# Three edits of the written order in an attention-and-MoE kernel: a first expert's last products ahead of the next one's transposes, a third expert's last weight loads behind its row transposes, and the last expert's row list held back longer in the plan

## The chip, the cores and the metric

The kernel runs on one core of a Trainium2 chip. The metric is the device time of one execution in microseconds (us); lower is better. The profiled execution has its own time, and a span from the first to the last recorded instruction inside it. Engines: PE is the matrix engine (PEld its weight loads), DVE, ACT and POOL are the vector, scalar and GpSimd engines, SP issues most DMAs.

## The reference

First attention over 8 batches of 8 heads, 576 positions, head size 64, with a causal mask in blocks of 64; then a mixture of experts over the 4608 rows of 512 that come out of it. Cut to what matters:

```python
scores = np.where(block_i >= block_j, scale * q @ k.T, -1e9)
x = softmax(scores) @ v                 # to rows: N=4608, D=512
logits = x @ w_gate                     # 8 experts
order = argsort(-logits.flatten())      # greedy, best pair first
# each row goes to one expert, each expert takes at most N // 8 = 576 rows
for e in range(8):
    h = np.maximum(x[rows_of_e] @ w1[e], 0.0)     # 512 -> 1024
    out[rows_of_e] = h @ w2[e]                    # 1024 -> 512
```

## The kernel before

The program is straight-line code whose order is written by a planner of its own, the class `Sched`. The parts of the work are Python generators that yield (engine, modelled duration, events waited for); the planner starts at each step the task that its model lets start first, by priority, and each start emits the instructions there and then. Engine letters are D, A, T, G, S for DVE, ACT, PE, POOL, SP. So a modelled time (`sc.soft`, `sc.dma`, `sc.ev`) changes no instruction, only the order in which each engine's queue holds them. On the chip every engine runs its queue in that order, and waits on real semaphores.

The first 370 us are attention, which ends with rows of x (an fp16 high part and an fp16 low part, 1024 numbers a row) in DRAM. Then eight experts follow, k = 0 to 7 in the order in which their capacity is filled. For each:

- `route(k)` searches the two bounds of the expert's logits in 14 steps: step t counts on DVE (`jk`, L776 and L777) and ACT (`ja`, L750), sums over the partitions on PE (`tot{k}_{t}`, L791), and goes on in DVE. It ends in masks MM, then `po{k}` on PE (L852 to L859), a row's place in the expert, and `invert`, which turns places into a list of rows: DVE makes h (L870), L (L872), OH (L893), OL (L897), RH (L899, L900), PE makes `pe{k}` (36 products, L908) and `ps{k}` (L915), DVE the index list `ix{k}`. `hold(k)` sets a modelled time before which the planner puts neither po nor pe into PE's order.
- `gather(k)` fetches the 576 rows by five indirect DMAs on POOL (`xg{k}_{m}`, L980; the fifth has 64 rows), and `flip` turns each into X{k}: for k < 2 eight PE transposes into a PSUM tile `xt{k}_{m}` (L990) and two copies (L994, L995), for k > 1 a transposing DMA on SP (L1005).
- `weights(k)` loads eight pieces of 512 KB per expert on SP (`raw{k}_1024_0` to `_3` of w1, `raw{k}_512_0`, `_2`, `_4`, `_6` of w2; L966; six buffers). A piece is scaled on ACT (L945), cut to its fp16 high part on ACT (L949), and the low part `W[:,1]` is made on POOL (L951).
- `ffn(k)` computes h on PE (L1030) as 8 column groups f for rows 0 to 255 and then for the others (`h{k}_{f}_{half}`), each of 12 products: d = 0 to 3, and for each d high by high, high by low rows, low weights by high rows. ACT and DVE cut h into HH and HL (L1016, L1018). Then `y{k}_{m}` (L1055; L1059 for the 64 rows of m = 4), in eight groups of three products of 512 columns (four of six for m = 4), ACT scales it (`yo`, L1038), and POOL scatters it to `out` (L1046). Two scatters write the same DRAM tensor, so that each waits for the landing of the one before.

Instructions of different experts interleave in each queue: the search of expert k+1 or k+2 runs beside the products of k, and the gathers, weight pieces and scatters of neighbouring experts share POOL's and SP's queues.

The lines that a reader needs beside the functions printed below are these of the planner:

```python
def soft(s, t, ev=None, lat=1100):
    s.q = max(s.q, s.now + lat) + t
    if ev:
        s.ev[ev] = s.q + 950
```

Of the kernel before, what the change touches and what calls it, by code (L numbers as in the profile page):

```python
# [16 lines left out]
D, A, T, G, S = "DATGS"  # L17
# [597 lines left out]
class Moe:  # L615
# [269 lines left out]
        yield from s.invert(k,L16,h2)  # L885
    def hold(s,k):

        s.sc.ev['hold',k]=s.sc.now+(8000 if k==s.E-1 else 0)
    def invert(s,k,L16,h2):
        nc=s.nc; rp=s.rp; C=s.C; V=nc.vector; sc=s.sc  # L890
        yield D,440
# [35 lines left out]
    def weights(s,k,eidx):  # L927

        nc=s.nc; wp=s.wp; sc=s.sc
        e=nc.sync.value_load(eidx[0:1,0:1],min_val=0,max_val=s.E-1)  # L930
        yield S,1000,('ffn',k-2)
        W=wp.tile([P,2,4,1024],F16,tag="W1",name=f"W1_{k}"); Y=wp.tile([P,2,8,512],F16,tag="W2",name=f"W2_{k}")
        s.W[k]=(W,Y)
        n=0; t0=sc.now
        def conv(n,raw,hi,lw,ev):
            if k<2 and n<4:
                yield A,947,('wl',k,n)
                nc.scalar.activation(hi,raw,AF.Copy,scale=s.WS)
                yield D,1135,('ix',k),('xm',0,0) if k==0 and n in s.XC else None
                nc.vector.scalar_tensor_tensor(lw,raw,s.WS,hi,op0=OP.mult,op1=OP.subtract)  # L940
            else:
                for h in range(2):
                    x=slice(512*h,512*h+512)
                    yield A,520,('wl',k,n)
                    nc.scalar.activation(raw[:,x],raw[:,x],AF.Copy,scale=s.WS)  # L945
                for h in range(2):
                    x=slice(512*h,512*h+512)
                    yield A,520
                    nc.scalar.activation(hi[:,x],raw[:,x],AF.Copy)  # L949
                yield G,2079  # L950
                nc.gpsimd.tensor_tensor(lw,raw,hi,op=OP.subtract)  # L951
            sc.set(ev)
        for dst,src,nd,wd in ((W,s.w1,4,1024),(Y,s.w2,8,512)):
            g=1024//wd
            for d in range(0,nd,g):
                if n>=6: yield S,25,'hw',('wc',k,n-6)
                elif k>0: yield S,25,'hw',('wc',k-1,n+2),('fl',1) if k==1 and n>=4 else None
                elif n==4:

                    yield G,60,('gi',0)  # L960
                    raw=wp.tile([P,1024],F32,tag="raw",name=f"raw{k}_{wd}_{d}",bufs=6)
                    nc.gpsimd.memset(raw[:,0:1],0.0)
                    yield S,25,'hw'
                else: yield S,25,'hw'
                if k or n!=4: raw=wp.tile([P,1024],F32,tag="raw",name=f"raw{k}_{wd}_{d}",bufs=6)
                nc.sync.dma_start(out=raw.rearrange("p (g f) -> p g f",g=g),in_=src[bass.ds(e,1),d*P:(d+g)*P,:].rearrange("o (g p) f -> p (o g) f",p=P))  # L966
                hi=dst[:,0,d:d+g].rearrange("p g f -> p (g f)"); lw=dst[:,1,d:d+g].rearrange("p g f -> p (g f)")
                sc.dma(1456,('wl',k,n))
                sc.add(conv(n,raw,hi,lw,('wc',k,n)),2,sc.now)
                n+=1  # L970
    WS=32.0; XS=64.0; NWU=8; NWM=0; GW=1; GS=2; XC=()
    def gather(s,k,ix):
        nc=s.nc; fp=s.fp; sc=s.sc
        tl=[]
        for m in range(5):
            n=P if m<4 else 64
            yield G,1038,('ffn',k-2),('xm',k-1,m)
            if m==0: X=s.X[k]=fp.tile([P,8,576],F16,tag="X",name=f"X{k}")
            xg=fp.tile([P,1024],F16,tag="xg",name=f"xg{k}_{m}",bufs=5)
            nc.gpsimd.indirect_dma_start(out=xg[:n],out_offset=None,in_=s.xd,in_offset=bass.IndirectOffsetOnAxis(ap=ix[:n,m:m+1],axis=0))  # L980
            sc.soft(728,('xg',k,m))
            sc.nolat()
            if m==4: sc.set(('gi',k))
            sc.add(s.flip(k,m,n,xg,X),1,sc.now)
# [138 lines left out]
```

## Time and profile before

| what | us |
|---|---|
| three timed executions, median (lowest to highest) | 804.21 (802.95 to 807.38) |
| the profiled execution | 801.86 |
| its span | 800.1 |
| PE busy in it | 717.8 (90%), 6539 products |
| DVE, ACT, POOL busy | 585.0, 545.1, 467.0 |
| DMA | 121.51 MB |

All rows are from the profiled execution, and their starts count from the start of its span. Matrix products are pipelined: a row's duration covers filling and draining, so that successive rows overlap, and the distance of the starts is what a product costs. The granted clock (PEclk) is a share of full speed: 1.00 is 2.4 GHz and 0.50 is 1.2 GHz.

### The profile page before, as it was taken

The page shows a single profiled execution, that of the slowest core. Times are in us where ns is not written, and L with a number is a line of the kernel's source. Part 1 is how long each engine was busy: PE and PEld are TensorE (multiplying, and loading weights), DVE is VectorE, ACT ScalarE, POOL GpSimd, SP SyncE. Part 2 cuts the span into 40 slices and gives each one's busy share as a digit, 9 for nine tenths or more (in the row PEclk, how much of TensorE's full clock was granted, in tenths as well). Part 3 has the DMA queues.
Part 4 walks back from the last instruction along what each step waited for, and adds up shares of the span by engine and source line. Part 5 has one row for each costly group of instructions (what it writes and reads, how often), then busy time and mean ns, then how long its engine had stood idle before and what let it go on. Part 6 is the DMA issues. An engine that isn't in the chain of part 4 may idle for free.

```text
span 800.1 us, 19136 instructions
## 1 busy us (share of the span) xinstructions
PE 717.8 (90%) x6539; PEld 479.6 (60%) x6539; DVE 585.0 (73%) x2395; ACT 545.1 (68%) x1476; POOL 467.0 (58%) x509
## 2 busy tenths in 40 slices
PE   5889998899999999913898999999999999999995
PEld 3666676677767767601644755747557475574752
DVE  6899798988889799488787977969777683730210
ACT  5789888888988888533745859496775947392210
POOL 5788888897889876212324337475471926873001
PEclk9899999999999999955899999999999999999998
DMA  9879999999999991324408049291845819861001
GB/s 203 157 145 179 213 203 209 164 176 204 230 164 222 188 198 35 99 80 133 138 14 294 25 139 231 74 295 42 254 129 184 179 49 273 270 162 40 20 15 45
DMA packets 244305, 121.51 MB, mean 152 GB/s; under 512 B 200816, under 2 KB 227312, under 8 KB 244208
## 3 DMA queue, kind: packets, MB, share of 16 engines
q1 hardware_dynamic: 238320, 101.42, 56.1%
q0 software_dynamic: 5888, 18.88, 7.4%
q8 instruction: 51, 0.84, 0.4%
q14 instruction: 46, 0.38, 0.2%
HBM read 71.32 MB, written 18.87 MB: 113 GB/s over the span
## 4 chain that ended last, share of the span: by engine, by line
PE 58%; DVE 19%; DMA 8%; ACT 8%; issue 3%; POOL 3%; SPq 1%; POOLq 0%; DVEq 0%; ACTq 0%
PE h L1030 23%; PE y L1055 16%; PE psb L463 5%; DVE m L405 5%; PE psb L380 4%; DMA kT<-k 4%; PE psb L498 4%; ACT P L416 4%; DVE kS L350 2%; POOL P L438 2%; PE y L1059 2%; DMA xg<-x,ix 2%; ACT PT L444 2%; DVE jk L776 1%; DMA raw<-in_moe_w_dram 1%
## 5 line engine op out<-in xcount | busy, mean ns | idle before, releaser
L438 POOL TENSOR_TENSOR P<-P,m 128x320 f32<-128x320 f32 (+8 forms) x285 | 209.3, 769 | 48.2 <-DVE m L430 28.4
L1030 PE MATMUL h<-X,W 128*128 128x320 f16 (+3 forms) x1536 | 195.1, 287 | 0.0
L1030 PEld LDWEIGHTS <-W 128*128 128x128 f16 x1536 | 142.2, 98 | 42.7 <-issue 3.1
L416 ACT ACTIVATE P<-psb,m 128x576 f32<-128x576 f32 (+8 forms) x288 | 149.2, 542 | 25.8 <-DVE m L409 19.7
L1055 PE MATMUL y<-W,HH 128*128 128x512 f16 x512 | 152.2, 379 | 0.0
L951 POOL TENSOR_TENSOR W<-raw,W 128x1024 f16<-128x1024 f32 x56 | 118.4, 2136 | 40.6 <-ACT W L949 38.3
L405 DVE TENSOR_REDUCE m<-psb 128x1 f32<-128x576 f32 (+8 forms) x288 | 125.0, 481 | 12.4 <-PE psb L380 11.9
L463 PE MATMUL psb<-mident,P 128*128 128x128 f32 x800 | 106.0, 281 | 10.9 <-POOL P L438 3.6
L1046 POOL DMA_INDIRECT out_dram<-yo,ix x40 | 39.4, 986 | 113.1 <-ACT yo L1038 79.2
L380 PEld LDWEIGHTS <-qT 128*64 128x64 f16 x1408 | 78.1, 112 | 42.8 <-issue 27.8
L380 PE MATMUL psb<-kT,qT 128*64 128x288 f16 (+8 forms) x704 | 91.7, 286 | 10.2 <-ACT P L416 9.7
L463 PEld LDWEIGHTS psb<-mident,P 128*128 128x128 f32 x800 | 87.3, 142 | 22.5 <-POOL P L438 6.4
L498 PE MATMUL psb<-PT,V 128*64 128x448 f32 (+5 forms) x776 | 97.2, 388 | 2.4 <-DVE PT L446 1.9
L980 POOL DMA_INDIRECT xg<-x,ix x40 | 41.6, 1040 | 95.8 <-DVE ix L918 37.7
L1055 PE MATMUL y<-W,HL 128*128 128x512 f16 x256 | 97.0, 379 | 0.0
L1016 ACT ACTIVATE HH<-h 128x320 f16<-128x320 f32 (+3 forms) x128 | 52.1, 410 | 63.9 <-PE h L1030 59.5
L444 ACT ACTIVATE PT<-psb 128x512 f32<-128x512 f32 (+1 forms) x165 | 82.4, 592 | 5.8 <-PE psb L463 5.6
L380 PE MATMUL psb<-kS,qT 128*64 128x288 f16 (+8 forms) x704 | 84.4, 284 | 1.6 <-DVE kS L350 1.5
L1018 DVE SCALAR_TENSOR_TENSOR HL<-h,HH 128x320 f16<-128x320 f32 (+3 forms) x128 | 56.9, 452 | 38.5 <-ACT HH L1016 38.2
L1055 PEld LDWEIGHTS <-HH 128*128 128x128 f16 x512 | 46.9, 98 | 52.6 <-issue 2.0
L945 ACT ACTIVATE raw<-raw 128x512 f32<-128x512 f32 x112 | 67.4, 626 | 6.6 <-DMA raw<-in_moe_w_dram 6.5
L498 PEld LDWEIGHTS psb<-PT,V 128*64 128x64 f32 x776 | 49.5, 137 | 33.5 <-issue 24.3
(204 smaller groups left out, 1074.9 us busy)
## 6 DMA issues: line engine op xcount, KB each, us to landing
raw<-in_moe_w_dram SPq DMA_DIRECT2D x64, 512.0 KB, 5.5
x<-XR SPq DMA_DIRECT2D x8, 1152.0 KB, 5.7
kn<-in_k_dram SPq DMA_DIRECT2D x15, 576.0 KB, 5.1
qn<-in_q_dram SPq DMA_DIRECT2D x15, 576.0 KB, 7.1
V<-in_v_dram SPq DMA_DIRECT2D x64, 128.0 KB, 4.4
V<-in_v_dram SPq DMA_DIRECT2D x16, 64.0 KB, 3.9
xg<-x,ix POOLq DMA_INDIRECT x40, 4.3
out_dram<-yo,ix POOLq DMA_INDIRECT x40, 2.8
```

Source lines behind the costliest of these rows:

```text
L380: nc.tensor.matmul(out if len(K1.shape) == 2 else out.rearrange("p (r j) -> p r j", r=2), lhsT=A[:, h, 64 * i:64 * i + 64], rhs=K1, start= ...
L405: nc.vector.tensor_reduce(m[:, 0, c:c + 1], ps[:, o:o + 64 * (i + 1)] if g else s.part(ps, g, i, o), axis=AX.X if g else AX.XY, op=OP.max)
L416: nc.scalar.activation(out, in_, AF.Exp, bias=m[:, 1, c:c + 1], scale=s.ESC, accum_out=m[:, 2, c:c + 1])
L438: nc.gpsimd.tensor_tensor(sl, sl, m[:, 3, c:c + 1].to_broadcast([P, w]), op=OP.mult)
L444: s.nc.scalar.activation(out, in_, AF.Copy)
L463: nc.tensor.transpose(ps[:, a], s.Pb[n % s.NP][:, s.OFF[i] + 128 * j:s.OFF[i] + 128 * j + P], s.ident)
L498: nc.tensor.matmul(ps[64 * h:64 * h + 64, 64 * (i0 - b0):64 * (b1 - b0)], lhsT=vn[:, j, 2 * (n % 2) + h, :], rhs=pt[:, s.PTI[(j, i0)]:s.PT ...
L945: nc.scalar.activation(raw[:,x],raw[:,x],AF.Copy,scale=s.WS)
L951: nc.gpsimd.tensor_tensor(lw,raw,hi,op=OP.subtract)
L1018: nc.vector.scalar_tensor_tensor(HL[:,f,ts],ps,0.0,HH[:,f,ts],op0=OP.max,op1=OP.subtract)
L1030: nc.tensor.matmul(ps,lhsT=W[:,a,d,f*P:f*P+P],rhs=X[:,4*(d//2)+d%2+l,ts],start=(d==0 and n==0),stop=(d==3 and n==2))
L1055: if m<4: nc.tensor.matmul(ps,lhsT=Z[:,f,m*P:m*P+P],rhs=Y[:,a,f],start=(f==n==0),stop=(f==7 and n==2))
```

## The change

Three places of the planner's input change; no instruction is added or removed. For the last expert `hold` grows from 8000 to 10000 ns. The loads of the third expert's last two pieces (n = 6, 7, that is `raw2_512_4` and `raw2_512_6`) wait in the plan for `('fl',2)`, set when the fifth transposing DMA of X2 is issued. And the planner's latency of the gathers of expert 1 becomes 4600 instead of 1100 ns. The line numbers after the third place are one higher in the changed kernel.

```diff
     def hold(s,k):
 
-        s.sc.ev['hold',k]=s.sc.now+(8000 if k==s.E-1 else 0)
+        s.sc.ev['hold',k]=s.sc.now+(10000 if k==s.E-1 else 0)
...
             for d in range(0,nd,g):
-                if n>=6: yield S,25,'hw',('wc',k,n-6)
+                if n>=6: yield S,25,'hw',('wc',k,n-6),('fl',2) if k==2 else None
...
             nc.gpsimd.indirect_dma_start(out=xg[:n],out_offset=None,in_=s.xd,in_offset=bass.IndirectOffsetOnAxis(ap=ix[:n,m:m+1],axis=0))
-            sc.soft(728,('xg',k,m))
+
+            sc.soft(728,('xg',k,m),4600 if k==1 else 1100)
```

The planner's order shifts from the entry of expert 1 on. Below, names are tiles with a running number behind them.

On PE, where expert 1 begins (xg1_0 is its first gathered piece, y0_3 and y0_4 the last two row groups of expert 0), this stands in the kernel before:

```order
L1055 MATMUL y0_3_6426<-W2_0_5524,HH0_5672 128x512
L1055 LDWEIGHTS HL0_5673
L1055 MATMUL y0_3_6426<-W2_0_5524,HL0_5673 128x512
L990 LDWEIGHTS xg1_0_6423
L990 MATMUL xt1_0_6498<-m_idh_130,xg1_0_6423 128x128
```

and this after it:

```order
L1056 MATMUL y0_3_6426<-W2_0_5524,HH0_5672 128x512
L1056 LDWEIGHTS HL0_5673
L1056 MATMUL y0_3_6426<-W2_0_5524,HL0_5673 128x512
L791 LDWEIGHTS m_bo_138
L791 MATMUL tot2_1_6503<-cn2_1_6480,m_bo_138 128x3
L1060 LDWEIGHTS HH0_5672
L1060 MATMUL y0_4_6505<-W2_0_5524,HH0_5672 64x512
```

Before, the transposes of xg1_0 come behind the seventh of the eight groups of y0_3, the eighth comes behind xt1_1, and the four groups of y0_4 are spread over the transposes up to h1_0_0. After, the eighth group of y0_3 and two groups of y0_4 stand ahead of xt1_0, the third between xt1_0 and xt1_1, the fourth ahead of xt1_2; xt1_3 is the last ahead of h1_0_0, and xt1_4 stands behind the first six products of h1_0_0.

On SP, behind the gathers of expert 2 (X2 is its transposed rows, the raw pieces are its last two; ISA is what goes with such a load), before:

```order
L1005 DMA_TRANSPOSE X2_7249<-xg2_0_7250 128x8x128
L966 ISA
L966 DMA raw2_512_4_7378<-in_moe_w2_dram 128x2x512
L1005 DMA_TRANSPOSE X2_7249<-xg2_1_7270 128x8x128
L966 ISA
L966 DMA raw2_512_6_7422<-in_moe_w2_dram 128x2x512
L1005 DMA_TRANSPOSE X2_7249<-xg2_2_7285 128x8x128
L1005 DMA_TRANSPOSE X2_7249<-xg2_3_7303 128x8x128
L1005 DMA_TRANSPOSE X2_7249<-xg2_4_7318 128x8x64
```

and after:

```order
L1006 DMA_TRANSPOSE X2_7252<-xg2_0_7253 128x8x128
L1006 DMA_TRANSPOSE X2_7252<-xg2_1_7273 128x8x128
L1006 DMA_TRANSPOSE X2_7252<-xg2_2_7288 128x8x128
L1006 DMA_TRANSPOSE X2_7252<-xg2_3_7306 128x8x128
L1006 DMA_TRANSPOSE X2_7252<-xg2_4_7321 128x8x64
L966 ISA
L966 DMA raw2_512_4_7493<-in_moe_w2_dram 128x2x512
L966 ISA
L966 DMA raw2_512_6_7497<-in_moe_w2_dram 128x2x512
```

The two loads have moved from behind the first and second transposing DMA to behind the fifth.

On POOL, from the first gather of expert 2 on (W1_2 and W2_2 are its weights, yo1_1 to yo1_3 the scatters of expert 1), before:

```order
L980 DMA xg2_4_7318<-x_61,ix2_7243 64x1024
L951 TENSOR_TENSOR W1_2_7109<-raw2_1024_0_7128,W1_2_7109 128x1024
L1046 DMA out_0_dram<-yo1_1_7287,ix1_6416 4608x512
L951 TENSOR_TENSOR W1_2_7109<-raw2_1024_1_7135,W1_2_7109 128x1024
L951 TENSOR_TENSOR W1_2_7109<-raw2_1024_2_7142,W1_2_7109 128x1024
L951 TENSOR_TENSOR W1_2_7109<-raw2_1024_3_7151,W1_2_7109 128x1024
L1046 DMA out_0_dram<-yo1_2_7366,ix1_6416 4608x512
L1046 DMA out_0_dram<-yo1_3_7461,ix1_6416 4608x512
L951 TENSOR_TENSOR W2_2_7110<-raw2_512_0_7156,W2_2_7110 128x1024
```

and after:

```order
L980 DMA xg2_4_7321<-x_61,ix2_7246 64x1024
L1047 DMA out_0_dram<-yo1_1_7290,ix1_6416 4608x512
L951 TENSOR_TENSOR W1_2_7112<-raw2_1024_0_7123,W1_2_7112 128x1024
L951 TENSOR_TENSOR W1_2_7112<-raw2_1024_1_7138,W1_2_7112 128x1024
L951 TENSOR_TENSOR W1_2_7112<-raw2_1024_2_7145,W1_2_7112 128x1024
L1047 DMA out_0_dram<-yo1_2_7359,ix1_6416 4608x512
L1047 DMA out_0_dram<-yo1_3_7439,ix1_6416 4608x512
L951 TENSOR_TENSOR W1_2_7112<-raw2_1024_3_7151,W1_2_7112 128x1024
L951 TENSOR_TENSOR W2_2_7113<-raw2_512_0_7162,W2_2_7113 128x1024
```

The five gathers stand as before. Behind them the scatter of yo1_1 has moved ahead of the conversion of raw2_1024_0, and that of raw2_1024_3 has moved from ahead of the scatters of yo1_2 and yo1_3 to behind both.

Further on, the order has these differences on the engines: tot3_6 stands ahead of h2_0_0 instead of within it; raw4_512_4 is issued ahead of X4_0 and raw4_512_6 ahead of X4_2; po7 stands three groups of y5 later, and pe7, which stood ahead of y5_4, stands behind y5_4 and the twelve products of h6_0_0; yo5_3 and yo5_4 are scattered ahead of the gathers of expert 7.

## Rows read from the trace of the kernel before

**Rows 1.** The page: PE's entry among the busy times of the span, and the shares of the span by engine in the chain that ended last.

```profile
PE 717.8 (90%) x6539; PEld 479.6 (60%) x6539; DVE 585.0 (73%) x2395; ACT 545.1 (68%) x1476; POOL 467.0 (58%) x509
...
PE 58%; DVE 19%; DMA 8%; ACT 8%; issue 3%; POOL 3%; SPq 1%; POOLq 0%; DVEq 0%; ACTq 0%
```

**Rows 2.** Two stretches of 20 us in the experts' part: length, then busy us (count) of PE, PEld, DVE, ACT and POOL, granted clock, DMA share, GB/s.

```profile
460.00:480.00 20.00, 20.00 (x161) 11.36 (x160) 16.00 (x82) 10.75 (x27) 7.01 (x5) 1.00 0.41 138
580.00:600.00 20.00, 19.41 (x136) 11.09 (x135) 15.26 (x91) 15.29 (x38) 15.83 (x10) 1.00 0.46 129
```

**Rows 3.** What PE waited for from 360 to 800 us: us in total, times, longest.

```profile
PE xt L990 <- DMA xg<-x,ix: 7.4, 6, 2.3
...
PE tot L791 <- ACT ja L750: 2.4, 3, 1.1
```

**Rows 4.** PE in order of time where expert 1 begins (some of its rows): start, duration, line, operation, count, and in brackets the idle time before and what ended it.

```profile
432.73 0.38 PE L1055 MATMUL y<-W,HL 128*128 128x512 f16 x1
...
434.86 0.62 PE L990 MATMUL xt<-m_idh,xg 128*128 128x128 f16 x8 [1.75 <-DMA xg<-x,ix]
...
436.29 0.62 PE L990 MATMUL xt<-m_idh,xg 128*128 128x128 f16 x8 [0.81 <-DMA xg<-x,ix]
...
438.53 0.62 PE L990 MATMUL xt<-m_idh,xg 128*128 128x128 f16 x8 [0.97 <-DMA xg<-x,ix]
...
440.12 1.03 PE L990 MATMUL xt<-m_idh,xg 128*128 128x128 f16 x16
...
443.63 1.81 PE L1030 MATMUL h<-X,W 128*128 128x256 f16 x15
```

**Rows 5.** POOL's fourth gather of expert 1, and the same DMA among the issues from 432.7 to 434.1 us (count, us from issue to landing).

```profile
432.95 0.95 POOL L980 DMA_INDIRECT xg<-x,ix  x1 [0.30 <-issue]
...
xg<-x,ix POOLq DMA_INDIRECT x1, 7.1
```

**Rows 6.** POOL in order of time behind the gathers of expert 2.

```profile
483.27 0.90 POOL L980 DMA_INDIRECT xg<-x,ix  x1 [0.30 <-DMA out_dram<-yo,ix]
484.19 2.15 POOL L951 TENSOR_TENSOR W<-raw,W 128x1024 f16<-128x1024 f32 x1
486.51 1.01 POOL L1046 DMA_INDIRECT out_dram<-yo,ix  x1 [0.17 <-ACT W L949]
487.55 6.32 POOL L951 TENSOR_TENSOR W<-raw,W 128x1024 f16<-128x1024 f32 x3
494.03 1.01 POOL L1046 DMA_INDIRECT out_dram<-yo,ix  x1 [0.17 <-issue]
499.55 0.96 POOL L1046 DMA_INDIRECT out_dram<-yo,ix  x1 [4.52 <-ACT HH L1016]
500.54 4.21 POOL L951 TENSOR_TENSOR W<-raw,W 128x1024 f16<-128x1024 f32 x2
```

**Rows 7.** Scatters to out: first the waiting instruction in POOL's queue from 484 to 506 us (durations min/median/max in ns, first and last start), then the scatters issued between 486 and 488, 494 and 495, 726 and 727 us, and the one at 422.7, with their us to landing.

```profile
L1046 POOLq EVENT_SEMAPHORE  x2: 17/30/43, 498.8 to 502.3; - x2
...
out_dram<-yo,ix POOLq DMA_INDIRECT x1, 5.3
...
out_dram<-yo,ix POOLq DMA_INDIRECT x1, 4.8
...
out_dram<-yo,ix POOLq DMA_INDIRECT x1, 2.7
...
out_dram<-yo,ix POOLq DMA_INDIRECT x1, 6.6
```

**Rows 8.** PE where h of expert 2 begins.

```profile
493.33 0.83 PE L1030 MATMUL h<-X,W 128*128 128x256 f16 x6
...
494.02 2.45 PE L1030 MATMUL h<-X,W 128*128 128x256 f16 x21
```

**Rows 9.** The start of the experts' part: stretches as in rows 2, and a row of PE inside them.

```profile
376.50:380.00 3.50, 0.79 (x10) 0.62 (x11) 2.39 (x5) 2.60 (x3) 2.89 (x3) 0.94 0.47 150
...
382.70:386.40 3.70, 3.70 (x38) 3.28 (x36) 0.93 (x8) 1.53 (x4) 0.00 (x0) 0.50 0.80 253
...
386.40:390.00 3.60, 2.48 (x42) 2.33 (x42) 3.41 (x22) 3.49 (x12) 0.00 (x0) 1.00 0.95 361
...
378.72 0.62 PE L990 MATMUL xt<-m_idh,xg 128*128 128x128 f16 x8 [2.33 <-DMA xg<-x,ix]
```

**Rows 10.** The making of expert 7's row list: DVE, POOL beside it, PE behind it, all h of expert 7 as a piece of the chain that ended last (start, us, what); the last row gives min/median/max ns of all eight instructions of L870.

```profile
680.55 5.25 DVE L870 TENSOR_SCALAR h<-q 128x36 f16<-128x36 f32 x1
...
686.41 5.38 DVE L897 TENSOR_TENSOR OL<-m_iom,L 128x1152 f16<-128x1152 f16 x1
...
679.46 6.30 POOL L951 TENSOR_TENSOR W<-raw,W 128x1024 f16<-128x1024 f32 x3
...
692.61 0.91 PE L908 MATMUL pe<-RH,OL 128*32 128x40 f16 x36 [1.35 <-DVE RH L900]
...
743.57 23.63 PE h L1030 x192
...
L870 DVE TENSOR_SCALAR h<-q x8: 173/182/5253, 369.1 to 680.5; 128x36 f16<-128x36 f32 x8
```

**Rows 11.** Step 6 of expert 5's search: ACT and PE.

```profile
585.42 0.63 ACT L945 ACTIVATE raw<-raw 128x512 f32<-128x512 f32 x1 [0.71 <-DMA raw<-in_moe_w_dram]
...
587.65 0.16 PE L791 MATMUL tot<-cn,m_bo 128*128 128x3 f16 x1 [0.58 <-ACT ja L750]
```

## The prediction

> **What bounds the kernel now.** I read the page first: PE is busy for 90% of the span and holds 58% of the chain that ended last [rows 1]. The slices by stage say more than that average: in the experts' part PE is busy for 19.4 to 20.0 of 20 us at a granted clock of 1.00 [rows 2]. So there the span is PE's queue read in order, and an edit of the order is worth the waits of PE that it takes away less those that it makes. The waits of PE come next: from 360 us on the largest is that of the transposes for gathered rows, 7.4 us in six waits, and one of the smaller is that of the search sums for ACT, 2.4 us [rows 3]. Of the 7.4, three waits lie at the entry of expert 1: 1.75 + 0.81 + 0.97 = 3.53 us [rows 4]. No row shows PE waiting for a low weight part at the entry of expert 2. That is the place to watch, because the change reorders POOL there.
>
> **The change, part by part.** No instruction is added, so each term is a wait that goes or comes.
>
> *Entry of expert 1 (gather latency 4600).* The transposes cannot run before their rows land. The fourth gather begins at 432.95 and is marked as landing 7.1 us after its issue, so at about 440.05 [rows 5]; its transposes begin at 440.12 today [rows 4]. The change can't move that. What it moves is work of y0: about 1.95 us (the eighth group of y0_3 and two groups of y0_4, 0.65 each) go ahead of the first transposes and fill the wait of 1.75; the other groups go into the next waits. Today the last two transposes (16 products from 440.12 on) are followed by three groups of y0_4, and h of expert 1 starts at 443.63. Afterwards nothing of y0 is left behind them. The 16 products end at about 441.1 (1.03 us from 440.12, with the last one's drain in it), so the 2.5 us of work that stood between 441.1 and 443.63 has gone into the waits: **-2.5 us**. The bounds: -3.0 if xt1_4, about half of the 16 products, hides inside h as well (h then starts at 440.65); -1.6 if the third wait, 0.97, is not filled.
>
> *Last loads of expert 2 behind its transposing DMAs.* Two loads leave about five entries of SP's queue later. Their low parts are read in the fifth and later groups of y2_0, behind all of h of expert 2; h alone is 96 products at 0.11 us (rows 8: 21 products and a search sum from 494.02 to about 496.34) and 96 wider ones, over 20 us. That covers two loads and their conversions: **0**. If the cover were gone, ACT would hold its queue for such a piece, and a sum of the search behind it would wait, as at 585.42, by 0.6 to 0.7 us [rows 11].
>
> *POOL at expert 2, which no diff line names.* This is the dear part. Today POOL ends the last gather at 484.17 (483.27 + 0.90), converts raw2_1024_0, scatters yo1_1 at 486.51, converts the other three pieces of w1 from 487.55 to 493.87, and only then scatters yo1_2 at 494.03; the scatter of yo1_3 starts at 499.55, after an idle time of 4.52 [rows 6]. The page puts that idle time on ACT's HH, but POOL's own queue shows what ended it: a wait of the scatter's line, released at 498.8 [rows 7], which is 494.03 plus the 4.8 us that the yo1_2 scatter took to land [rows 7], and 0.72 us later the next one starts. Nothing needed POOL in those 4.52 us, so today they cost nothing. The twelfth product of h2_0_0 is the first to read raw2_1024_3's low part. h begins at 493.33 with six products, six more come from 494.02 at 0.11 each [rows 8], so it starts at 494.57, 0.7 us after the conversion's end.
>
> Afterwards the same wait stands *ahead* of that conversion. With starts counted on the clock of before: a group of y1 (three products, 0.65 us) more stands ahead of pe2, so the gathers end at 484.8; yo1_1 ends at 486.1; three conversions of 6.32 together end at 492.5; yo1_2 is scattered at 492.65; it lands 5.05 later (the mean of the scatters at 486.51, 5.3, and 494.03, 4.8 [rows 7]) at 497.7; the wait passes 0.72 later at 498.4; the scatter of yo1_3 takes 1.0; the conversion takes 2.1 (4.21 / 2 [rows 6]) and ends at 501.5; PE goes on at 501.6. Against 494.57 that is a stall of **+7.0 us**. All of h2 and y2 is queued behind that product on PE, and nothing can pass it. The bounds are the quickest and the slowest landing in rows 7: 2.7 gives 4.65, 6.6 gives 8.6. I take the middle since the two neighbours in the same traffic are the nearest rows.
>
> For this landing the Trainium skill has a rule ("DMA: Bandwidth & Descriptors", section "Anatomy of one DMA — SWDGE (gpsimd) path"): a DMA that GpSimd issues takes about 2.0 us plus its bytes over 436 GB/s, for the 262,144 bytes of a scatter an estimate of 2.6 us. The scatter between 726 and 727 us, in a quiet stretch, agrees with 2.7; the two in this traffic, with 5.3 and 4.8, do not. By the rule the stall would be 4.6 and the sum 2.4 lower.
>
> *What the stall does to the clock.* At the start of the experts' part PE was busy 0.79 of 3.50 us, with a wait of 2.33 for gathered rows; then it ran 3.70 us without a gap at a granted 0.50, and from 386.40 at 1.00 again [rows 9]. After 7 us of nothing I expect the same: 3.7 us of work at half clock do 1.85 us of full-clock work: **+1.85**. Bounds: 0 if the clock stays, and +3.4 if the fall lasts nearly twice as long.
>
> *The last expert (hold 10000).* pe7 waits 1.35 us for RH, because DVE's h took 5.25 us and OL 5.38 while POOL converted, where the median of h is 0.18 [rows 10]. pe7 moves behind y5_4 (four groups, 2.6 us) and twelve products of h6_0_0 (1.3), 3.9 in all. po7 moves 1.95 us back (three groups), and DVE's chain with it at most as far: 1.35 + 1.95 - 3.9 is below zero, so the wait goes: **-1.35**. Bounds: 0 (DVE held by 1.35 longer beside POOL) to -1.35. The row list is then some 2.6 us later; h of expert 7 begins at 743.57, 50 us behind [rows 10], which hides it.
>
> *Expert 5's search.* PE waits 0.58 for ACT's count at 587.65, since ACT waited 0.71 for a weight piece [rows 11]. raw4_512_6 is issued earlier in the new order: **-0.5**, bounds 0 to -0.6.
>
> **The sum.** -2.5 + 7.0 + 1.85 - 1.35 - 0.5 = **+4.5 us**. On the profiled execution's own 801.86 (span 800.1 and 1.76 around it) that is 806.4. Its time lies 2.35 below the median of the three timed ones, 804.21; on that median the sum gives **808.7 us**, which I forecast. About 0.5%, 4.0 us, is what a measurement of this kernel can tell from no change.
>
> **The rivals.**
> - *Quick landing, or the clock stays.* With a landing of 2.7 the stall is 4.65 and the sum +2.15 (806.4); with the clock staying at 1.00 and the middle landing it is +2.65 (806.9); with both +0.3 (804.5). For it: the quiet landing [rows 7], and yo1_2 is scattered 1.4 us earlier, in other traffic. Against: both neighbours, and the fall in rows 9 came after a shorter wait. The Trainium skill's rule above stands on this side.
> - *The scatter doesn't wait.* Its idle time of 4.52 is put down to ACT [rows 6]. If that were the real releaser, yo1_3 would follow yo1_2 at once: 492.65 + 1.0 + 1.0 + 2.1 = 496.8, a stall of 2.2 without a fall of the clock, and a sum of -2.15: 802.1, not slower. It decides at a landing below about 1 us. Against: the wait is released at 498.8, which is 494.03 + 4.8.
> - *The gains alone.* If expert 2's rows are asked for so much earlier against PE that the conversion still ends by 494.6, the sum is -4.35: 799.9, faster. POOL would have to be 7 us ahead; its first gather hangs on the index list, which hangs on PE's order. Little speaks for it.
> - *Slower still.* A landing of 6.6 (+1.6), the longer fall (+1.5), or a late last piece that holds ACT and a search sum (+0.7) and the first term at its bound (+0.9): 811 to 813.
>
> **How the numbers follow.** Forecast with +3.4 to +6: 0.47; slower still 0.10; quick landing or steady clock 0.27; the scatter doesn't wait 0.09; gains alone 0.07. About 0.07 of the first case is under 4.0. Slower: 0.40 + 0.10 = 0.50. Same: 0.07 + 0.27 + 0.09 = 0.43. Faster: 0.07. The range is 802.5 to 812.5: it leaves out the gains alone, half of the case at 802.1 and half of the slower still. The likeliest case alone runs from 807.6 to 810.2.
>
> **What the new profile would show.** Right: PE's h line begins expert 1 with no three waits before it; one wait of 6 to 8 us on L1031 in h2_0_0, released by POOL's W, with two scatters before that conversion and the second idle for about 5 us; a granted clock near 0.5 for some 4 us behind; pe7 without a wait. Wrong: a wait under 3 us there, or a granted clock of 1.00 through it; or a new wait at a search sum of expert 2 or 3 larger than 1 us.

## The result, and the profile after

The changed kernel took 810.28 us (median of 8, 808.05 to 814.64), the kernel before 804.35 beside it (median of 8): ratio 1.0076, 95% interval 1.0054 to 1.0099, slower by about 6.1 us. The profiled execution of after took 810.03 with a span of 808.3, 8.2 over that of before.

The engines' busy times, from the page of after, answer to [rows 1]:

```profile
PE 719.6 (89%) x6539; PEld 479.9 (59%) x6539; DVE 584.7 (72%) x2395; ACT 546.1 (68%) x1476; POOL 466.5 (58%) x509
```

PE does the same work (the same number of products, 1.8 us more of busy time), so the 8.2 us are waits and a lower clock. What PE waited for from 360 us on (us in total, times, longest), against [rows 3]:

```profile
PE h L1031 <- POOL W L951: 6.3, 1, 6.3
...
PE xt L991 <- DMA xg<-x,ix: 4.7, 4, 2.2
...
PE tot L791 <- ACT ja L750: 2.9, 2, 1.8
```

The wait that the prediction asked for is there, one of 6.3 us for POOL's conversion, which before does not have. That for gathered rows fell from 7.4 to 4.7 and that for ACT's counts rose from 2.4 to 2.9.

The entry of expert 1 on PE, against [rows 4]: the transposes of the third and fourth gather and the first products of h1; those of the fifth follow inside h1.

```profile
438.76 0.62 PE L991 MATMUL xt<-m_idh,xg 128*128 128x128 f16 x8 [0.26 <-DVE cd L769]
...
440.43 0.62 PE L991 MATMUL xt<-m_idh,xg 128*128 128x128 f16 x8 [1.05 <-DMA xg<-x,ix]
...
440.92 0.81 PE L1031 MATMUL h<-X,W 128*128 128x256 f16 x6
```

h1 starts 2.7 us earlier than at 443.63, although y0 began 0.4 us later. Only 0.26 and 1.05 of waiting are left.

POOL behind the gathers of expert 2, against [rows 6]; then the us to landing of the scatter issued at 490.79 and the waiting instruction of the scatter's line in POOL's queue from 488 to 500 us, against [rows 7]:

```profile
484.31 6.31 POOL L951 TENSOR_TENSOR W<-raw,W 128x1024 f16<-128x1024 f32 x3
...
490.79 1.00 POOL L1047 DMA_INDIRECT out_dram<-yo,ix  x1 [0.17 <-issue]
...
497.02 0.96 POOL L1047 DMA_INDIRECT out_dram<-yo,ix  x1 [5.23 <-DMA raw<-in_moe_w_dram]
...
498.00 6.29 POOL L951 TENSOR_TENSOR W<-raw,W 128x1024 f16<-128x1024 f32 x3
```

```profile
out_dram<-yo,ix POOLq DMA_INDIRECT x1, 5.5
...
L1047 POOLq EVENT_SEMAPHORE  x2: 17/30/43, 496.3 to 499.8; - x2
```

The second scatter starts 0.73 us after the first has landed (490.79 + 5.5 = 496.29), after 5.23 us of nothing. The row puts that idle time on the landing of a weight piece, but POOL's own queue passes its wait at 496.3, which is the landing of the scatter. The conversion of raw2_1024_3 is the first of the three from 498.00 on. PE beside it, against [rows 8]:

```profile
492.44 0.18 PE L791 MATMUL tot<-cn,m_bo 128*128 128x3 f16 x1 [0.93 <-DVE jk L777]
...
492.48 1.36 PE L1031 MATMUL h<-X,W 128*128 128x256 f16 x11
...
500.19 0.39 PE L1031 MATMUL h<-X,W 128*128 128x256 f16 x1 [6.34 <-POOL W L951]
```

Eleven products of h2_0_0 are done, the twelfth waits 6.34 us. The 0.93 ahead of it is a search sum, tot3_6, which now stands before h2_0_0. The clock in the same stretch (length, busy us of PE, PEld, DVE, ACT and POOL, granted clock, DMA share, GB/s), against [rows 9]:

```profile
495.50:496.00 0.50, 0.00 (x0) 0.00 (x0) 0.00 (x0) 0.00 (x0) 0.00 (x0) 1.00 1.04 406
...
496.00:496.50 0.50, 0.00 (x0) 0.00 (x0) 0.00 (x0) 0.00 (x0) 0.00 (x0) 0.51 0.73 283
...
500.20:506.00 5.80, 5.80 (x30) 4.12 (x31) 3.40 (x21) 3.86 (x10) 5.01 (x3) 0.50 0.03 7
...
506.00:506.50 0.50, 0.50 (x5) 0.41 (x4) 0.50 (x5) 0.50 (x2) 0.00 (x0) 0.75 0.93 213
```

It falls at 496.0 with PE idle, and stays at half until 506.25. PE works through the last 5.80 us before 506 without a gap at 0.50: 2.9 us lost, and 0.1 in the half microsecond behind. At the start of the experts' part before, the whole stretch at half clock, of which [rows 9] have the last 3.70 us, was this:

```profile
379.57:386.40 6.83, 5.52 (x51) 4.84 (x52) 2.88 (x11) 2.53 (x6) 2.33 (x3) 0.50 0.72 213
```

The last expert, against [rows 10]: a run of conversions on POOL, DVE's h, pe7 on PE, and the RH that it needs on DVE.

```profile
690.20 6.31 POOL L951 TENSOR_TENSOR W<-raw,W 128x1024 f16<-128x1024 f32 x3
...
692.01 4.55 DVE L870 TENSOR_SCALAR h<-q 128x36 f16<-128x36 f32 x1
...
704.84 0.91 PE L908 MATMUL pe<-RH,OL 128*32 128x40 f16 x36
...
702.92 0.39 DVE L900 TENSOR_SCALAR RH<-OH,m_pc 128x720 f16<-128x720 f16 x1
```

RH is there at 703.3 and pe7 starts at 704.84, behind twelve products of h6, without a wait. And the search of expert 6: ACT takes up a weight piece, and tot6 behind it.

```profile
637.88 0.63 ACT L945 ACTIVATE raw<-raw 128x512 f32<-128x512 f32 x1 [2.50 <-DMA raw<-in_moe_w_dram]
...
639.63 0.16 PE L791 MATMUL tot<-cn,m_bo 128*128 128x3 f16 x1 [1.77 <-ACT ja L750]
```

ACT waited 2.50 us for raw5_512_4, and PE 1.77 for the count queued behind it; before, it was 0.72 at the same place (ACT 1.04).

Summed from the starts of h and y of each expert in the two traces, after less before: up to y0 +0.4; y0 to h1 -3.1; h1 to y1 +0.85 (the last transposes and a search sum inside h1); y1 to h2 +1.0 (tot3_6); h2 to y2 +9.2 (6.3 of wait, 2.9 of clock); y3 to h4 -0.2; y4 to h5 +1.3; y5 to y6 -1.3; the rest 0. That is 8.2.

### The profile page after: what moved, and what is told of

It is laid out like the page before. It is cut to its first block, busy times and chain, and to the rows that moved or that the text cites. A ratio compares the mean times of both kernels' runs of the same rounds, so it can differ in the third digit from the quotient of the medians.

```text
span 808.3 us, 19130 instructions
## 1 busy us (share of the span) xinstructions
PE 719.6 (89%) x6539; PEld 479.9 (59%) x6539; DVE 584.7 (72%) x2395; ACT 546.1 (68%) x1476; POOL 466.5 (58%) x509
## 4 chain that ended last, share of the span: by engine, by line
PE 58%; DVE 17%; DMA 9%; ACT 7%; POOL 5%; issue 4%; SPq 0%; POOLq 0%; DVEq 0%; ACTq 0%
PE h L1031 22%; PE y L1056 16%; PE psb L463 5%; DVE m L405 5%; PE psb L498 4%; PE psb L380 4%; ACT P L416 3%; DMA kT<-k 3%; PE y L1060 2%; DMA raw<-in_moe_w_dram 2%; DVE kS L350 2%; POOL P L438 2%; ACT PT L444 2%; DVE jk L776 1%; DMA xg<-x,ix 1%
## 5 line engine op out<-in xcount | busy, mean ns | idle before, releaser
L1031 PE MATMUL h<-X,W 128*128 128x320 f16 (+3 forms) x1536 | 198.8, 289 | 6.3 <-POOL W L951 6.3
L380 PE MATMUL psb<-kS,qT 128*64 128x288 f16 (+8 forms) x704 | 82.6, 280 | 1.6 <-DVE kS L350 1.5
```

Source lines behind the costliest of these rows:

```text
L380: nc.tensor.matmul(out if len(K1.shape) == 2 else out.rearrange("p (r j) -> p r j", r=2), lhsT=A[:, h, 64 * i:64 * i + 64], rhs=K1, start= ...
L1031: nc.tensor.matmul(ps,lhsT=W[:,a,d,f*P:f*P+P],rhs=X[:,4*(d//2)+d%2+l,ts],start=(d==0 and n==0),stop=(d==3 and n==2))
```

## The experiments

Each ratio is to the kernel before, run beside it on the same chip. The runs came in three groups (the first and third on one chip, the second on another), and before itself took 803.4, 806.8 and 810.5 us in them, so kernels are compared within a group.

**First group (e1 to e4): which edit costs, and by which mechanism.**

e1, edit three alone:

```diff
-            sc.soft(728,('xg',k,m))
+            sc.soft(728,('xg',k,m),4600 if k==1 else 1100)
```

> Edit three alone (the planner's gather latency of expert 1 is 4600), the other two undone. Theory: the whole loss comes with this edit, through POOL's order at expert 2, so the wait of 6.3 us for raw2_1024_3's low part at h2_0_0 and the half clock behind it (about 3 us more) stay; only the wait of pe7, 1.35 us, comes back. Time 1.3 us above the changed kernel, 7 us above the kernel before, ratio 1.006 to 1.011. Rival (the two loads of expert 2, moved behind the transposing DMAs, or the row list of expert 7, held longer, cost part of it): 0 to 5 us under the changed kernel, ratio below 1.004, and the wait at h2_0_0 shorter or gone.

Measured: 816.0 us, ratio 1.016 (1.0132 to 1.0188), above the expected range. Two waits of PE from its trace:

```profile
500.81 1.03 PE L1030 MATMUL h<-X,W 128*128 128x256 f16 x4 [7.09 <-POOL W L951]
...
703.07 0.92 PE L908 MATMUL pe<-RH,OL 128*32 128x40 f16 x36 [1.27 <-DVE RH L900]
```

The wait at h2_0_0 is there at 7.09, and pe7's is back at 1.27. So edit three carries the loss. But its ratio is 0.8% over that of the changed kernel, where 1.3 us (0.17%) was expected. The profiled execution, the quickest of the five at 812.3, shows a search sum of expert 4 that waits 1.15 us for ACT, which is not all of the difference; the third group takes this up.

e2, edits one and two without edit three (the diff of e1 undone in the changed kernel).

> Edits one and two (hold 10000, the two loads of expert 2 behind its transposing DMAs), edit three undone. Theory: POOL's order at expert 2 is that of before, no wait for a low weight part at h2_0_0; the wait of pe7 for RH goes (1.35 us), the three waits at expert 1's entry (3.5 us) stay: 1 to 2 us under the kernel before, ratio 0.997 to 0.999. Rival (the moved loads hold ACT, and with it search sums): a wait of PE at a search sum of expert 2 to 4 over 1 us that the kernel before does not have, ratio above 1.001.

Measured: 801.25 us, ratio 0.9982 (0.9960 to 1.0003). The first transposes at expert 1's entry, and pe7:

```profile
435.59 0.62 PE L990 MATMUL xt<-m_idh,xg 128*128 128x128 f16 x8 [1.77 <-DMA xg<-x,ix]
...
695.33 0.92 PE L908 MATMUL pe<-RH,OL 128*32 128x40 f16 x36
```

The waits at the entry stay and pe7's is gone; there is no wait at h2_0_0, and behind expert 1's entry no search sum waits over 0.4 us. The two edits are worth about what was expected (2.1 us by the medians), though the interval reaches 1.

e3, the changed kernel with one scatter moved:

```diff
-            yield G,1038,('yo',s.ny-1),('gi',1) if k==0 and m>1 else None
+            yield G,1038,('yo',s.ny-1),('gi',1) if k==0 and m>1 else None,('wc',2,3) if k==1 and m==3 else None
```

> All three edits, and the scatter of yo1_3 put behind the conversion of raw2_1024_3 in POOL's queue; that of yo1_2 stays ahead of it. Theory (POOL's wait for the landing of yo1_2 before it can scatter yo1_3 is what delays the conversion): one scatter alone costs its 1.0 us, the conversion ends about 493.95 on the changed kernel's clock where PE wants it at 493.85; wait of 0 to 0.3 us, granted clock 1.00 there, 9.2 us under the changed kernel's profile, so 1 to 3 us under the kernel before, ratio 0.996 to 0.999. Rival (the 5.2 us were a wait for ACT or for yo1_3, or the scatters themselves hold the conversion up): a wait of 2 us or more stays, ratio 1.000 to 1.005.

Measured: 802.3 us, ratio 0.9985 (0.9962 to 1.0009). POOL with the scatter of yo1_2 and two conversions (raw2_1024_3's first; that of yo1_3 follows at 495.78); PE's twelfth product; and the clock from 495 to 500:

```profile
490.36 1.00 POOL L1046 DMA_INDIRECT out_dram<-yo,ix  x1 [0.17 <-issue]
...
491.39 4.22 POOL L951 TENSOR_TENSOR W<-raw,W 128x1024 f16<-128x1024 f32 x2
...
493.59 1.27 PE L1030 MATMUL h<-X,W 128*128 128x256 f16 x10 [0.17 <-POOL W L951]
...
495.00:500.00 5.00, 5.00 (x49) 4.48 (x48) 4.89 (x29) 4.75 (x13) 2.29 (x3) 1.00 0.35 135
```

One scatter still stands ahead of the conversion and costs its 1.0 us; with the second behind, POOL no longer sits out the landing, PE waits 0.17 instead of 6.34, and the clock stays at 1.00. That one line takes 9.2 us off the span of the profile (808.3 to 799.1), 9.0 of them between the starts of h2 and y2, and the ratio is 0.9985 instead of 1.0076. This settles the mechanism. Of the expected 1 to 3 us under before there were 1.1. What was left are waits like these, from 480 to 800 us, PE's for counts and ACT's for weight pieces:

```profile
PE tot L791 <- ACT ja L750: 2.4, 5, 0.9
...
ACT raw L945 <- DMA raw<-in_moe_w_dram: 6.4, 6, 2.5
```

e4, the scatters spread so that the wait would be shorter:

```diff
+        m2={2:('ys',1,2),3:('ys',1,3),4:('wc',2,3)}
-                yield G,2079
+                yield G,2079,m2.get(n) if k==2 else None
-            yield G,1038,('yo',s.ny-1),('gi',1) if k==0 and m>1 else None
+            yield G,1038,('yo',s.ny-1),('gi',1) if k==0 and m>1 else None,('wc',2,m-1) if k==1 and m in (2,3,4) else None
+            sc.ev['ys',k,m]=sc.now
```

> All three edits, with the scatters spread: yo1_2 between the conversions of raw2_1024_1 and _2, yo1_3 between _2 and _3. The wait for the landing of yo1_2 then begins 2.1 us earlier: theory on the changed kernel's clock: yo1_2 scattered at 488.7, landed 5.2 later, yo1_3 at 494.6, conversion of raw2_1024_3 until 497.7, so a wait of PE of 3.9 instead of 6.3 us. On the clock there are two claims. Claim one: the clock falls to half here too (in the changed kernel it fell at 496.0, 2.2 us after PE's last product) and the products behind lose another 3 us: 2.4 us under the changed kernel, ratio 1.004 to 1.006. Claim two: only the longer gap brings it down, and the granted clock stays 1.00: 5.4 us under the changed kernel, ratio 1.000 to 1.002.

Measured: 812.34 us, ratio 1.0099 (1.0069 to 1.0129), above both claims. The planner put two more search sums ahead of h2's products, so the wait was not shortened but cut in pieces:

```profile
493.70 0.18 PE L791 MATMUL tot<-cn,m_bo 128*128 128x3 f16 x1 [0.93 <-DVE jk L777]
...
496.05 0.19 PE L791 MATMUL tot<-cn,m_bo 128*128 128x3 f16 x1 [2.18 <-DVE jk L777]
...
497.87 0.19 PE L791 MATMUL tot<-cn,m_bo 128*128 128x3 f16 x1 [0.96 <-DVE jk L777]
...
494.50:495.00 0.50, 0.00 (x0) 0.00 (x0) 0.50 (x4) 0.50 (x3) 0.50 (x1) 0.64 0.78 291
...
642.21 0.16 PE L791 MATMUL tot<-cn,m_bo 128*128 128x3 f16 x1 [3.65 <-ACT ja L750]
...
642.00:648.00 6.00, 5.79 (x16) 2.12 (x16) 1.93 (x14) 4.41 (x11) 4.02 (x3) 0.50 0.42 115
```

Three search sums wait 0.93, 2.18 and 0.96 with little between them (a search sum, then three products), and the clock falls at 494.6 and is back at 501.5. So the clock falls around waits of which none was longer than 2.2 us, and no clean 3.9 us wait was made there.

The same trace has one elsewhere: a search sum of expert 6 waits 3.65 us for ACT. The clock falls at 641.4, inside that wait, and is back at 648.2; PE worked 6.0 us at half, 3.0 us lost, as much as behind 6.34 us in the changed kernel. That is what claim one said of a wait of this length.

**Second group (e5 to e8): the clock, the last row list, a better version.**

e5, one conversion more ahead of the one that PE needs:

```diff
-                yield G,2079
+                yield G,2079,('wc',2,4) if k==2 and n==3 else ('ys',1,3) if k==2 and n==4 else None
+            sc.ev['ys',k,m]=sc.now
```

> All three edits, and the conversion of raw2_512_0 (2.1 us on POOL) put ahead of that of raw2_1024_3 as well, so that everything that PE waits for at h2_0_0 comes 2.1 us later still: a wait of 8.4 us instead of 6.3. What the clock takes behind it: claim one, the half clock lasts about 6 us from PE's return whatever the wait was, so 3.0 us again: 2.1 us above the changed kernel, ratio 1.009 to 1.012. Claim two, the loss grows with the wait (2.95 x 8.4 / 6.3 = 3.9): 3.1 us above it, ratio 1.011 to 1.014.

Measured: 816.68 us, ratio 1.0105 (1.0076 to 1.0134). POOL's second scatter, and two waits of PE:

```profile
497.54 0.96 POOL L1046 DMA_INDIRECT out_dram<-yo,ix  x1 [5.62 <-DMA raw<-in_moe_w_dram]
...
487.94 0.16 PE L791 MATMUL tot<-cn,m_bo 128*128 128x3 f16 x1 [1.85 <-ACT ja L750]
...
502.79 1.46 PE L1030 MATMUL h<-X,W 128*128 128x256 f16 x6 [2.75 <-POOL W L951]
```

PE goes on 5.25 us after the start of the second scatter instead of 3.17, the 2.1 of one conversion: confirmed. The wait of 8.4 us was not made: again search sums had moved ahead of it (they wait 0.93, 2.18 and 0.32), and 2.75 was left at h2_0_0; 1.85 us of the time is a wait for ACT that has nothing to do with it. So this run does not tell the two claims on the clock apart. The 3.65 us of e4, with the same 3.0 us lost as behind 6.34, speak against a loss that grows with the wait; for a wait over 6.34 us it stays open.

e6, edits two and three without edit one (hold back at 8000).

> Edits two and three, hold back at 8000. Theory (from the run with edit three alone, 5.7 us above the changed kernel: the two loads issued between the transposing DMAs make the scatter of yo1_2 land later and hold ACT in the next search): with the loads behind, the landing is 5 to 5.5 us, the wait at h2_0_0 6.0 to 6.5, no search sum of expert 4 waits over 0.5 us, and only the wait of pe7, 1.3 us, comes on top of the changed kernel: 811.6, ratio 1.008 to 1.011. Rival (hold is what makes the difference): 814 to 816, ratio 1.013 to 1.018.

Measured: 818.2 us, ratio 1.0137 (1.0108 to 1.0166): nearer to the rival. PE's wait at pe7:

```profile
710.36 0.92 PE L908 MATMUL pe<-RH,OL 128*32 128x40 f16 x36 [2.62 <-DVE RH L900]
```

It is 2.62 instead of the expected 1.3, with the granted clock at 1.00 behind it (709 to 718 us). The wait at h2_0_0 was 2.67, not 6.0 to 6.5, and four search sums of experts 3 to 6 waited 1.1 to 2.1 us, so the theory's account fails on these three points. It was repeated beside the changed kernel as e12.

e7, the kernel of e3 with ACT's late pieces planned later:

```diff
                 sc.dma(1456,('wl',k,n))
+                if n>=6 and 1<k<7: sc.ev['wl',k,n]+=4000
```

> The kernel with the scatter of yo1_3 behind the conversion, and the planner's landing time of the last two pieces of experts 2 to 6 set 4 us later, so that ACT takes them up behind the next counts of the search. Theory (what keeps that kernel from its gain is ACT waiting for such a piece with a search sum behind it, 0.89 + 0.46 + 0.28 + 0.46 + 0.27 = 2.4 us on PE): most of these waits go, about 2 us less, ratio to the kernel before 0.994 to 0.997. Rival (the pieces are then late for y, or the counts move and wait for DVE instead): no change or worse, ratio above 0.998.

Measured: 803.66 us beside 806.77, ratio 0.995 (0.9928 to 0.9972): faster than before, and by its ratio than the changed kernel. PE's waits for counts from 480 us on, and ACT's longest wait that is put down to no instruction of the core:

```profile
PE tot L791 <- ACT ja L750: 2.7, 2, 2.0
...
ACT yo L1039 <- remote: 2.1, 1, 2.1
```

No piece of weights holds ACT behind 480 us any more (6 waits, 6.4 us in all, in e3). The two waits for counts that are left, 2.03 and 0.67, have another cause: just ahead of them ACT stood still for 2.1 and 1.4 us, which the trace puts down to no engine or DMA of the core (`remote`).

e8, the same line added to e2's kernel.

> Edits one and two without edit three, with the same later landing time of the last two pieces. Theory: only one wait of 0.4 us at a search sum is left to take, so 0 to 0.5 us under the run without edit three, ratio 0.997 to 0.998; the difference to the run with edit three and its scatter behind is then what edit three is worth by itself, 3.1 us at the entry less 0.9 and 1.0 us given back before h of expert 2, 1.2 us. Rival (other waits appear): ratio above 0.999.

Measured: 804.08 us, ratio 0.9964 (0.9938 to 0.9989). Between e8 and e7 lies 0.4 us, not the 1.2 expected, and well inside the intervals. So edit three, freed from what it does to POOL, gains nothing that can be told here.

**Third group (e9 to e12): the changed kernel taken apart on one chip.**

e9 is the changed kernel, e10 edit three alone (the kernel of e1), e11 edits one and three, e12 edits two and three (the kernel of e6).

> The changed kernel once more, beside the three that follow, since runs taken at different times gave 0.8% between it and edit three alone, where 1.3 us (0.17%) was expected. Expected: ratio 1.0054 to 1.0099 as before. If the wait at h2_0_0 is set by the landing of yo1_2, it moves with the landing: 6.3 us for 5.5, one for one.

> Edit three alone, once more beside the changed kernel. Theory one (edits one and two together are worth 3 to 6 us once edit three is in: 1.3 from pe7, the rest from loads that no longer land beside the scatter and in the searches of experts 3 to 5): 3 to 6 us above the changed kernel. Theory two (the 0.8% came from the state of the memory at the time of the runs): 1 to 2 us above it.

> Edits one and three, the two loads of expert 2 back between its transposing DMAs (edit two undone). Theory one: 2 to 4.5 us above the changed kernel, the wait at h2_0_0 over 6.8 us since the loads lengthen the landing of yo1_2 to over 6, and search sums of expert 4 waiting for ACT. Theory two (edit two costs and brings nothing, as forecast): within 1 us of the changed kernel.

> Edits two and three, hold at 8000 (edit one undone), once more beside the changed kernel; the orders of the two differ only around the last expert. Forecast's term: pe7's wait of 1.3 us and nothing else, 1 to 2 us above the changed kernel. If it is 4 us or more, holding the last row list back does more than take that wait away.

| run | edits | median us | ratio to before (95% interval) |
|---|---|---|---|
| e9 | 1, 2, 3 | 814.77 | 1.0055 (1.0030 to 1.0080) |
| e10 | 3 | 817.12 | 1.0077 (1.0051 to 1.0104) |
| e11 | 1, 3 | 813.67 | 1.0038 (1.0018 to 1.0058) |
| e12 | 2, 3 | 820.51 | 1.0115 (1.0089 to 1.0142) |

e9 came out as expected by its ratio, but not the wait: the landing of yo1_2 rose from 5.5 to 6.0 us, and PE went on 3.18 us after the second scatter's start as before (3.17), yet PE waited 4.72 and not 6.8, since a search sum that waited 1.88 beside y1 had brought it to the place later. e10 lies 2.35 us above e9, between its two theories. e11 lies 1.1 below, against its theory one.

The start of yo1_3's scatter and the idle time before it, of e9, e10, e11, e12 in turn:

```profile
498.58 0.96 POOL L1047 DMA_INDIRECT out_dram<-yo,ix  x1 [5.80 <-DMA raw<-in_moe_w_dram]
...
500.13 0.96 POOL L1046 DMA_INDIRECT out_dram<-yo,ix  x1 [6.91 <-DMA X<-xg]
...
498.95 0.96 POOL L1046 DMA_INDIRECT out_dram<-yo,ix  x1 [6.75 <-DMA X<-xg]
...
498.44 0.96 POOL L1046 DMA_INDIRECT out_dram<-yo,ix  x1 [5.00 <-DMA raw<-in_moe_w_dram]
```

With the two loads behind the transposing DMAs (e9, e12) POOL's idle time is 5.80 and 5.00, with them between (e10, e11) 6.91 and 6.75. In these traces edit two shortens POOL's idle time by about 1 to 2 us, yet the times do not follow: e9 is 1.1 us over e11, e12 3.4 over e10. So edit two brings nothing; e12 and e10 differ at pe7, too, which waits in e12 alone. Edit one is worth 5.7 us (e12 less e9) and 3.5 us (e10 less e11, with intervals that overlap), not 1.3. The trace of e12 shows where most of the first of the two goes: POOL's conversions, DVE's h, pe7, and the clock around it.

```profile
697.41 6.29 POOL L951 TENSOR_TENSOR W<-raw,W 128x1024 f16<-128x1024 f32 x3
...
697.26 6.50 DVE L870 TENSOR_SCALAR h<-q 128x36 f16<-128x36 f32 x1
...
710.56 0.92 PE L908 MATMUL pe<-RH,OL 128*32 128x40 f16 x36 [2.59 <-DVE RH L900]
...
709.00:712.00 3.00, 1.44 (x42) 0.98 (x42) 1.71 (x4) 0.00 (x0) 1.26 (x2) 1.00 0.80 267
...
712.00:715.00 3.00, 3.00 (x26) 1.34 (x24) 0.17 (x1) 0.00 (x0) 1.78 (x2) 0.57 0.52 173
...
715.00:718.00 3.00, 3.00 (x26) 1.94 (x23) 0.68 (x1) 0.98 (x2) 2.12 (x3) 0.86 0.75 240
```

DVE's h took 6.50 us where [rows 10] have 5.25, pe7 waited 2.59, and the clock, at 1.00 through a wait of 1.35 in before, fell to half: mean 0.57 and 0.86 over two stretches of 3 us are 3.4 us at half, 1.7 us lost. From y5 to y6 e12 is 5.1 us longer than e9, and 4.3 of that are this wait and the clock behind it. So edit one takes away 1.3 us in before, and in e12 over 4. The length of the wait does not decide the clock's part: in e6, the same program, 2.62 us brought no fall. The 3.5 us between e10 and e11 are not explained: in the one profile of e10 pe7 did not wait. There OL, which took 5.38 us beside POOL's conversions in before [rows 10], took 0.75, and POOL's next conversions began only at 703.12, 2.1 us after it.

The same program (e1, e10) was at 1.016 in one group and 1.0077 in another on the same chip: it took 816.0 and 817.1 us, and before 803.4 and 810.5, so it was mostly before that moved. A ratio of one group is therefore not held against that of another to better than about 0.8%; that e3 removes the loss rests on its trace as well. The profiles of the second and third groups, all but that of e9, show waits of 1.2 to 5.3 us on ACT and DVE that the trace puts down to nothing on the core; those of the first group, of after and of before have none. What they are was not tried.

## Why the prediction was right

The time, 810.28, lies in the range, and the direction and mechanism are those forecast. That it came within 1.6 us of the 808.7 is in part luck: the two timed medians lie 5.9 us apart and the two profiles 8.2, and the profiled execution, for which the sum gave 806.4, took 810.03. By its steps:

- **Entry of expert 1, -2.5.** The start of h1 moved by -3.1 against y0, of which 0.85 came back inside h1, about 0.4 of it as the transposes of the fifth gather and 0.28 as the wait of a search sum: -2.2 up to y1. Right within its bounds. What the step left out is tot3_6, which now stands ahead of h2_0_0 and waits for DVE, 0.93, just under the 1 us that the prediction named as a sign of being wrong. The order showed it, and the prediction does not price it. It comes ahead of the stall and shortens it, so the two together are 7.3.
- **POOL at expert 2, +7.0.** 6.34 measured, and every stage of the working is in the rows: landing 5.5 (5.05 taken), 0.73 to the next scatter (0.72), conversion 2.1. The landing made it 0.45 longer, and it came out shorter all the same because PE reached the place about 1.1 us later against y1 than the sum had it, most of that by tot3_6 (0.93). Shown by e3 to be the cause. The rival "the scatter doesn't wait" fell with it, and so did the 2.7 us landing.
- **The clock, +1.85.** 2.9 to 3.0 measured: the step was mis-sized. I took the 3.70 us of unbroken work in [rows 9] as the time at half, but in before the half clock had begun at 379.57, with broken work ahead of that. PE worked 5.52 us at half in all there, which would have given +2.8; in after it worked some 6 us at half. Of the numbers in the prediction its upper bound, +3.4, came nearest.
- **Loads of expert 2, 0.** Right by e9 against e11: the landing of yo1_2 is 6.0 us in e9 and 7.0 in e11, and that did not reach the time.
- **pe7, -1.35.** -1.33 in the profiles of before and after: right there. In e6 and e12 the same wait is 2.6 us, and in e12 the clock fell behind it, so the term holds for the wait of before and not for every run of that order.
- **Expert 5's search, -0.5.** The 0.58 is gone as said, but the next search pays 1.77 where it paid 0.72: +1.1 for the two by the starts of h. The step failed by following a piece only to the sum next to it and not to the same place one expert later.

The sum came to +4.5, the profile to +8.2 and the timed ratio to 6.1. The errors in the wait and the clock nearly cancel (8.85 against 9.2, +0.4). The rest of the 3.7 is what the entry gave back up to h2 (-1.2 in place of -2.5: +1.3), the searches of experts 5 and 6 (+1.1 in place of -0.5: +1.6) and a later start of the experts' part (+0.4).

## What to carry to other kernels

When an edit shifts one engine's order, compare the order of all engines before pricing it: here the dear line was a scatter that moved past a conversion on a queue that no edit named. A wait that costs nothing (4.52 us on POOL) becomes a stall once something that another engine needs is queued behind it; moving one such instruction took 9.2 us off the span. Price a wait of PE together with the half clock that can follow it: 3.0 us behind waits of 3.65 and of 6.34 here.

## What the runs showed of the hardware

The granted clock fell from 1.00 to 0.50 about 2.2 us into a full stop of PE (493.8 to 496.0) and came back some 6 us after PE resumed. In e4 it fell at 494.6, behind a wait of 0.93, one search sum, and 0.8 us into a wait of 2.18, and again at 641.4, 2.9 us into a wait of 3.65, to come back 6.0 us after PE resumed. In e12 it fell with PE at work again, 1.9 us behind a wait of 2.59. It did not fall behind the 2.62 of pe7 in e6, a wait of 2.17 at a search sum in e8, the 1.35 of pe7 in before, or the three waits of 1.75, 0.81 and 0.97 at expert 1's entry there. So in these runs the length of a wait alone does not tell whether the clock falls.

The DVE instruction that makes h is 0.18 us elsewhere [rows 10]. In before it ended at 685.80 and POOL's run of three conversions at 685.76; in after 696.56 and 696.51; in e12 703.76 and 703.70. So three times it came to its end 0.04 to 0.06 us behind POOL's last conversion, whenever it had begun; in before and after its length is how much of POOL's run was left. The Trainium skill ("SBUF — State Buffer", section "SBUF: two separate sides") tells of a port pair for which DVE and GpSimd hold an exclusive lock, each for a whole instruction. The rows agree in that DVE stands still, and add that it did not get in between three instructions that follow each other. A DVE instruction that held such a lock from its own start would not have waited, yet in e12 h had begun 0.15 us ahead of POOL's run by these records and still ended behind it. Why, and whether it is this port pair at all, no run here shows.
